# Lower halves of the k and v loads issued from GpSimd's queue instead of SyncE's

## Chip, cores and metric

The kernel runs on one core of a Trainium2 chip. The metric is the device time of one launch in microseconds (us); lower is better. A core has TensorE (PE in the profile), VectorE (DVE), ScalarE (ACT), GpSimd (POOL) and SyncE (SP). Each of the five has its own instruction queue, worked in order. A DMA is issued by an instruction in one of these queues; the transfer itself is done by the core's 16 DMA engines.

## The reference, cut to what matters

All inputs are bf16. There are 2048 tokens of D = 640 channels; x is `A_q`.

```python
# branch A: a long convolution over the tokens
k_shift = sum(k_pad[:, t:t+S, :] * shift_k[:, 3 - t] for t in range(4))
kv = k_shift * v
y  = irfft(rfft(pad(kv)) * rfft(pad(ssm_k)))[:S] + kv * ssm_D
a  = q * y
# branch B: a mixer over four shifted column groups, then an MLP
h  = gelu(layernorm(x) @ w1)          # 640 -> 640
x1 = x + shifted(h) @ w2
b  = x1 + gelu(layernorm(x1) @ w3) @ w4   # 640 -> 1536 -> 640
# the gate
g   = sigmoid((x * gate_w).sum(-1, keepdims=True))
out = g * a + (1 - g) * b
```

## The kernel before

**Work and tiling.** The 2048 tokens are cut into 16 slices s = 0 to 15 of 128 partitions. A partition of the lower half (0 to 63) and one of the upper half (64 to 127) hold different token ranges, so that a load of token rows is written as two DMAs of 64 partitions each. The helper `halves` (line 378) does this: it makes one task that issues the upper half (g = 1) and then the lower half (g = 0), both from SP (line 382). The loads of x (`ldx`), k (`ldk`), v (`ldv`), q (`ldq`) and most stores go through it.

**Branch A.** The shifted k times v is worked out on DVE in four groups of four slices, kv3, kv2, kv1, kv0 in this order (lines 870 to 894). A group has four taps (a product of a window of K with a row of shift_k, line 878), three sums (line 882) and the product with v (line 886, called kv3.v to kv0.v here), all on 128 x 2560 elements in bf16. K is one buffer of 19 slices that holds all of k: its pieces are loaded by `ldk15`, `ldk11`, `ldk7`, `ldk3` (lines 554 to 556; the number is the first of four slices) and two smaller loads. A group takes its windows from its own piece and the one ahead of it: kv3 from K15 and K11, kv2 from K11 and K7, kv1 from K7 and K3. The product with v is written back into K. v has one buffer for all four groups (slot 0 of VC, line 871), so that the load of V2 can only start when kv3.v has read V3, and so on: `ldv3` waits for nothing on DVE, `ldv2` waits for kv3.v, `ldv1` for kv2.v, `ldv0` for kv1.v. The long convolution is a two-step Fourier transform by matmuls: step 1 for the filter (h, line 911) and for kv (x, line 913), evictions of PSUM into FS (lines 387 and 389), stores to DRAM scratch (line 943), loads back (FX, line 957), step 2 (line 965), products (line 980), the way back (lines 993, 1005, 1019, 1031). Step 1 of kv for slices 0 to 3 is the last of its kind and needs kv0.v.

**Branch B.** Layernorm statistics of x (`st1`, DVE or ACT) and their last part on POOL (`rs1`, lines 594 to 597: a power of -0.5 among others), normalization (`nm1`, lines 601 and 631), transposes, w1 (lines 689, 693), gelu (706), w2 (715), x1 (722), then the second layernorm: sums of squares on ACT (`sq`, line 727), `ve2` (lines 775 to 777 on POOL, or 779 and 780 on DVE) and `st2` (lines 785 to 787, always POOL) per pair of slices, `nm2` (lines 601 and 603) per slice, a transposing DMA (`dt2`, line 808), w3 (817), gelu (824), w4 (833, 842), and the sum with the residual (850). The name st2.2 means st2 of the pair of slices 2 and 3; nm2.2 is the normalization of slice 2, and it needs st2.2.

**What sets the order.** Every piece of work is a task with the engine that it runs on, the buffers that it reads and writes, and what it takes from small pools. A string (`ORDER`, line 37) lists all task numbers by hand in the order in which they are emitted; an engine's queue holds its instructions in this order. Semaphore waits are put in from what each instruction reads and writes. DMAs issued from SP take eight completion semaphores in turn, so that an SP issue also waits until the one eight before it on SP has landed.

On POOL the order before is: constants, `rs1` for slices 5, 4, 1, 0, 14, 3, 2, 15, `cjp` (the copy at line 389 that brings shift_k into rows), `rs1` for 9, 7, 6, 8, `dfold` (line 865), `rs1` for 11, 12, 13, 10, then ve2.0, st2.0, ve2.2, st2.2, ve2.4, st2.4, ve2.6, st2.6, st2.10, st2.8, st2.14, ve2.12, st2.12. On DVE, nm2.2 stands directly behind kv3.v and ahead of the first tap of kv2; nm2.4 and nm2.7 stand behind kv0.v.

Of the kernel before, what the change touches and what calls it, by code (L numbers as in the profile page):

```python
# [83 lines left out]
class Plan:  # L84
# [13 lines left out]
    def add(self, name, eng, dur, fn, r=(), w=(), use=(), acq=(), rel=(), roles=(), after=(), mode=None, nbytes=0):  # L98
        eng = dict(eng) if isinstance(eng, dict) else {eng: dur}
        t = Task(len(self.tasks), name, eng, fn)  # L100
        t.mode, t.bytes, t.roles, t.after = mode, nbytes, roles, after
        t.kept = None
        t.acq = [(a, 1, a == "U") if isinstance(a, str) else a for a in acq]
        t.rel = [(x[0], x[1], x[2] if len(x) > 2 else None) for x in rel]
        for k in r:
            if k in self.writer:
                t.deps |= self.writer[k]
            self.readers.setdefault(k, set()).add(t.idx)
        for k in w:
            t.deps |= self.writer.get(k, set()) | self.readers.pop(k, set())  # L110
            self.writer[k] = {t.idx}
        for o in use:
            t.deps.add(o.idx)
        t.deps.discard(t.idx)
        self.tasks.append(t)
        return t
# [238 lines left out]
def build(env, nc, io):  # L355
# [22 lines left out]
    def halves(name, nbytes, out, in_, **kw):  # L378

        def fn(t):  # L380
            for g in (1, 0):
                nc.sync.dma_start(out=out(t, g), in_=in_(t, g))  # L382
        return add(name, "SP", 1.08, fn, nbytes=nbytes, **kw)

    def copy(t, out, in_):
# [115 lines left out]
    def c_bm(t):  # L501
        for g in range(2):
# [8 lines left out]
                                                  in_=io["sk"].rearrange("d j -> (d j)").unsqueeze(0)), w=["CJR"], roles=("VC",))  # L511
# [6 lines left out]
                                                           in_=env.CD[:].broadcast_to([P, 4 * D])), r=["CD"], w=["CJP"] + [("CJ", j) for j in range(4)], roles=("VC",))  # L518
# [20 lines left out]
    for s0, n in ((2, 2), (4, 2), (6, 4), (0, 2), (14, 2), (10, 4)):  # L539
        halves(f"ldx{s0}", P * n * D * BF * (HALF if n < 4 else 1.05), lambda t, g, s0=s0, n=n: env["x"][64 * g:64 * g + 64, s0:s0 + n, :],  # L540
               lambda t, g, s0=s0, n=n: qv[g, :, s0:s0 + n, :], w=[("x", s, g) for s in range(s0, s0 + n) for g in range(2)])
# [3 lines left out]
                                                     in_=io["w2"].rearrange("(q r) n -> r q n", q=4)[0:128]),  # L545
        w=["W2a"], roles=("W12",))
    for q in range(4):
        dma(f"ldw2b{q}", 40960, lambda t, q=q: nc.sync.dma_start(out=env["W12"][32 * q:32 * q + 32, 1, 4, :],
                                                                 in_=io["w2"][160 * q + 128:160 * q + 160, :]),
# [4 lines left out]
    for i0 in (15, 11, 7, 3):  # L554
        halves(f"ldk{i0}", P * 4 * D * BF * 1.05, lambda t, g, i0=i0: env["K"][64 * g:64 * g + 64, i0:i0 + 4, :],
               lambda t, g, i0=i0: kv_[g, :, i0 - 3:i0 + 1, :], w=[("K", i, g) for i in range(i0, i0 + 4) for g in range(2)], roles=("K",))
# [62 lines left out]
    for s0 in pairs:  # L619
# [16 lines left out]
        if s0 in DMA1:  # L636
            for s, n in zip((s0, s0 + 1), nm):
                dma(f"dt1.{s}", P * D * BF * 1.8, lambda t, s=s, n=n: nc.sync.dma_start_transpose(
                    out=env["xnT"][:, s + 2, :, :], in_=env["xn"][:, n.buf["xn"][0], :]), issue=1.25, use=[n], rel=[(n, "xn")],
# [29 lines left out]
    for G in (1, 0, 2, 3):  # L669
        a = 4 * G  # L670
        owner = None
        for part in (3, 1, 0, 2, 4) if G == 0 else (2, 0, 1, 3, 4):
# [6 lines left out]
            def w1(t, a=a, fbs=fbs):  # L679
# [6 lines left out]
                for b, fb in enumerate(fbs):  # L686
# [9 lines left out]
            t = add(f"w1.{G}.{part}", "PE", 1.1, w1, r=["W1"] + [("xnT", s) for s in sorted(need)] +  # L696
                    [("xnTz", z) for z in (-2, 16) if z in need or z + 1 in need], use=[owner] if owner else [], acq=[ONE] if owner else [ONE, "hs"],
                    mode="f" if part < 4 else "c32", roles=("xnT", "W12"))
# [11 lines left out]
        for s in range(a, a + 4):  # L710
            def w2(t, s=s, o=owner):
                m = env.Uf(t.buf["U"][0])
                for (c0, c1) in ((0, 512), (512, 640)):
# [3 lines left out]
            t = add(f"w2.{s}", "PE", 1.38, w2, r=["W2a"] + [("W2b", q) for q in range(4)] + [("hs", G, p) for p in range(5)],  # L717
                    rel=[(owner, "hs")], acq=("U",), mode="f", roles=("W12", "hsT"))
# [75 lines left out]
    for c in range(4):  # L794
# [18 lines left out]
        for fb in range(12):  # L813
            def w3(t, fb=fb, nP=nP):
                for kb in range(5):
# [3 lines left out]
            t = add(f"w3.{c}.{fb}", "PE", 1.09, w3, r=["W3"] + [("x1nT", 4 * c + i) for i in range(4)], rel=[(nT, nP)],  # L819
                    use=[h2] if h2 else [], acq=[ONE] if h2 else [ONE, "h2"], after=("xnT",), mode="c64" if c == 3 else "f")  # L820
# [5 lines left out]
        for s in range(4 * c, 4 * c + 4):  # L826
# [19 lines left out]
            t = add(f"w4.{s}", "PE", 3.28, w4, acq=("U",), **kw)  # L846
# [7 lines left out]
    for cb in range(5):  # L854
# [5 lines left out]
        t = add(f"trh.{cb}", "PE", 1.0, trh, r=["ID", ("SK", cb)], use=[fill], acq=("U",), mode="f", roles=("SK",))  # L860
# [9 lines left out]
    for gi in (3, 2, 1, 0):  # L870
        halves(f"ldv{gi}", P * 4 * D * BF * 1.05, lambda t, g: env["VC"][64 * g:64 * g + 64, 0, :, :],
               lambda t, g, gi=gi: vv[g, :, 4 * gi:4 * gi + 4, :], w=["V"], roles=("VC",))
# [79 lines left out]
    for m in range(10):  # L952
        own, e2 = {}, {}
        for which in "hx":
# [5 lines left out]
            for pc in range(2):  # L960
                def mm(t, ld=ld, pc=pc):
                    X = env["FX"][:, ld.buf["FX"][0], :]
                    for j in range(4):
# [5 lines left out]
                t = add(f"s2{which}.{m}.{pc}", "PE", 0.22, mm, use=[ld] + ([o] if o else []), r=["TRIG"], rel=[(ld, "FX")],  # L969
                        acq=("U",) if o else ("U", pool), mode="q32", after=("VC",), roles=("FX",))  # L970
# [24 lines left out]
        t = add(f"s3.{m}", "PE", 0.88, back, use=[pa, pb], rel=[(pa, "PP")], acq=[("U", 1, True), ("U", 1, True)], mode="s32", roles=("PP",))  # L995
# [19 lines left out]
        out=env["BT"][:], in_=env.BP.rearrange("p s t -> p (s t)")), issue=1.25, r=["BP"], w=["BT"])  # L1015
    for s0 in range(0, 16, 2):
        def rg(t, s0=s0):
# [4 lines left out]
                      lambda t, g, s0=s0: qv[g, :, s0:s0 + 2, :], acq=("Q",), w=[("q", s0)], after=("W12",))  # L1022
        oown = None
        for i in range(2):
# [8 lines left out]
            t = add(f"s4.{s}", "PE", 0.29, mm, use=[ld], r=["BT"], rel=[(ld, "GX")], acq=("U",), mode="c64")  # L1033
# [36 lines left out]
        if s0 in LATE:  # L1070
            continue
        halves(f"st.{s0}", P * 2 * D * BF * 1.3, lambda t, g, s0=s0: ov[g, :, s0:s0 + 2, :],
               lambda t, g, o=oown: env["QO"][64 * g:64 * g + 64, 4 + 2 * o.buf["O"][0]:6 + 2 * o.buf["O"][0], :],
# [33 lines left out]
```

## Time and profile before

| | us |
|---|---|
| median of 3 plain runs | 225.13 (224.52 to 225.18) |
| the profiled execution | 227.05 |
| its span, first to last instruction | 225.3 |
| ACT busy | 154.4 |
| POOL busy | 45.8 |
| idle ahead of DVE's first tap | 2.06 |

The profiled execution is one run, some 2 us longer than the median; the span leaves out what lies ahead of the first instruction and behind the last. TensorE's granted clock was 1.000 on this core. Over the whole span 57.94 MB are moved at a mean of 257 GB/s; SP's queue carries 57.27 MB of it in 39158 packets, 89.9% of the time of 16 DMA engines. POOL issues no DMA. In a row of a timeline the columns are the start, the time of the row (both in us), the engine, the line, the operation with what it writes and reads, the count, and in brackets the idle time ahead of it with what ended it. "SPq" is SP's queue, whose instructions are DMA issues; "us to landing" is the time from issue to landing. In the rows of stages, the columns behind an engine's busy time in brackets are instruction counts; the last three are TensorE's granted clock, the share of the 16 DMA engines' time, and GB/s.

### The profile page before, as it was taken

To read this page: it belongs to the slowest core of one execution; us is meant where nothing else is said; L and a number is where in the kernel's file an instruction comes from. 1 tells how busy PE (TensorE), PEld (TensorE's weight loads), DVE (VectorE), ACT (ScalarE), POOL (GpSimd) and SP (SyncE) were. 2 spreads that over 40 slices of the span, in tenths; PEclk is the share of its full clock that TensorE was granted. 3 is DMA by queue.
4 is the path that set the end of the run, shared out by engine and by line. 5 is a ranking of instruction groups with operands and counts; after the bars stand their busy time and mean duration, and the time that the engine had idled before them with its cause. 6 is when DMAs were issued, how large, how long until landed. Compare 5 with 4: busy or idle time off the path is not lost.

```text
span 225.3 us, 5381 instructions
## 1 busy us (share of the span) xinstructions
PE 212.7 (94%) x2161; PEld 106.4 (47%) x2178; DVE 189.3 (84%) x281; ACT 154.4 (69%) x225; POOL 45.8 (20%) x86
## 2 busy tenths in 40 slices
PE   3999889899999999999999999999999999999992
PEld 1576454466444444345543433334444555555561
DVE  7998896999999999997469989899857426989984
ACT  6998969799988999889658988888675002225000
POOL 7481532436200009930710000000000000000000
PEclk9999999999999999999999999999999999999999
DMA  6999999999999998979899989999992596988624
GB/s 193 281 308 232 220 237 238 327 233 327 349 240 287 241 272 252 379 270 270 193 367 311 373 154 285 316 304 309 247 255 88 185 374 209 281 250 249 203 64 116
DMA packets 39503, 57.94 MB, mean 257 GB/s; under 512 B 15027, under 2 KB 30645, under 8 KB 39478
## 3 DMA queue, kind: packets, MB, share of 16 engines
q1 hardware_dynamic: 39158, 57.27, 89.9%
q10 hardware_dynamic: 320, 0.33, 0.5%
q8 instruction: 17, 0.28, 0.5%
q14 instruction: 8, 0.07, 0.1%
HBM read 35.56 MB, written 18.36 MB: 239 GB/s over the span
## 4 chain that ended last, share of the span: by engine, by line
PE 63%; DMA 17%; DVE 12%; SPq 3%; issue 2%; ACT 1%; DVEq 0%
PE PS L817 18%; PE PS L833 17%; PE PS L715 9%; DMA x<-in_A_q_dram 7%; PE PS L965 5%; DMA W<-in_B_w_dram 4%; PE PS L689 4%; PE PS L993 4%; DMA SK<-in_A_ssm_k_dram 3%; DVE VC L878 3%; DVE VC L882 3%; DMA QO<-in_A_q_dram 2%; SPq L382 2%; PE PS L911 2%; PE PS L1031 1%
## 5 line engine op out<-in xcount | busy, mean ns | idle before, releaser
L824 ACT ACTIVATE h2T<-PS 128x512 bf16<-128x512 f32 x48 | 27.9, 605 | 27.3 <-PE PS L817 26.9
L833 PE MATMUL PS<-W,h2T 128*128 128x512 bf16 (+3 forms) x306 | 39.8, 298 | 0.3
L387 ACT CAST FS<-PS 128x1024 bf16<-128x1024 f32 x37 | 36.0, 1021 | 5.4 <-PE PS L913 3.5
L817 PEld LDWEIGHTS <-W 128*128 128x128 bf16 (+1 forms) x300 | 22.1, 103 | 29.4 <-issue 8.4
L833 PEld LDWEIGHTS <-h2T 128*128 128x128 bf16 (+1 forms) x312 | 22.4, 100 | 18.5 <-issue 1.6
L387 ACT CAST XH<-PS 128x1024 bf16<-128x1024 f32 x26 | 25.5, 1020 | 7.5 <-PE PS L965 7.4
L817 PE MATMUL PS<-x1nT,W 128*128 128x512 bf16 x120 | 28.5, 380 | 0.0
L817 PE MATMUL PS<-XB,W 128*64 128x512 bf16 (+1 forms) x180 | 28.5, 380 | 0.0
L980 DVE TENSOR_TENSOR PP<-XH 128x2048 bf16<-128x2048 bf16 x20 | 23.6, 1219 | 3.1 <-ACT XH L387 2.8
L878 DVE TENSOR_TENSOR VC<-K,VC 128x2560 bf16<-128x2560 bf16 x16 | 23.7, 1490 | 2.3 <-DMA W<-in_B_w_dram 2.1
L715 PE MATMUL PS<-W,hsT 128*128 128x128 bf16 (+1 forms) x155 | 23.5, 297 | 0.9 <-DMA W<-in_B_w_dram 0.6
L850 DVE TENSOR_TENSOR x<-PS,x 128x640 bf16<-128x640 f32 x12 | 9.8, 823 | 13.4 <-PE PS L833 13.2
L689 PE MATMUL PS<-xnT,W 128*128 128x512 bf16 x80 | 19.2, 379 | 0.1
L715 PEld LDWEIGHTS <-hsT 128*128 128x128 bf16 x160 | 12.8, 98 | 13.0 <-issue 1.1
L882 DVE TENSOR_TENSOR VC<-VC 128x2560 bf16<-128x2560 bf16 x12 | 17.9, 1489 | 0.3
L389 DVE CAST XH<-PS 128x1024 bf16<-128x1024 f32 x14 | 16.9, 1220 | 1.2 <-PE PS L965 1.1
L1037 DVE SCALAR_TENSOR_TENSOR W<-PS,GG,QO 128x640 bf16<-128x640 f32 x16 | 13.6, 877 | 2.4 <-PE PS L1031 1.9
L387 ACT CAST GS<-PS 128x1024 bf16<-128x1024 f32 x12 | 12.0, 1016 | 3.9 <-PE PS L993 3.9
L255 PE MATMUL PS<-C 128*128 128x512 bf16 x34 | 9.9, 434 | 3.8 <-DVE C L506 3.7
L842 PE MATMUL PS<-W,h2T 128*64 128x512 bf16 (+1 forms) x192 | 13.4, 299 | 0.0
L722 DVE SCALAR_TENSOR_TENSOR x<-PS,x 128x640 bf16<-128x640 f32 x16 | 12.8, 815 | 0.1
L965 PE MATMUL PS<-FX,TRIG 64*32 64x512 bf16 x320 | 12.4, 381 | 0.3 <-ACT GS L387 0.3
(115 smaller groups left out, 294.0 us busy)
## 6 DMA issues: line engine op xcount, KB each, us to landing
FH<-FS SPq DMA_DIRECT2D x8, 640.0 KB, 6.3
FXD<-FS SPq DMA_DIRECT2D x8, 640.0 KB, 5.0
FX<-FH SPq DMA_DIRECT2D x10, 512.0 KB, 6.0
FX<-FXD SPq DMA_DIRECT2D x10, 512.0 KB, 5.3
GX<-GD SPq DMA_DIRECT2D x8, 640.0 KB, 5.9
W<-in_B_w_dram SPq DMA_DIRECT2D x2, 1920.0 KB, 11.9
GD<-GS SPq DMA_DIRECT2D x8, 480.0 KB, 4.0
SK<-in_A_ssm_k_dram SPq DMA_DIRECT2D x5, 512.0 KB, 6.5
```

The source lines that it names most:

```text
L387: nc.scalar.copy(out=out, in_=in_)
L389: (nc.vector if t.on == "DVE" else nc.gpsimd).tensor_copy(out=out, in_=in_)
L689: nc.tensor.matmul(m[:, b, :], lhsT=W[:, 0, kb, 160 * fb:160 * fb + 128], rhs=rhs(kb, shifts[fb]), start=(kb == 0), stop=(kb == 4))
L715: nc.tensor.matmul(m[:, c0:c1], lhsT=env["hsT"][:, o.buf["hs"][0], fb, 128 * (s % 4):128 * (s % 4) + 128], rhs=env["W12"][:, 1, fb, c0:c1] ...
L817: nc.tensor.matmul(env.PS[q:q + w, t.buf["U"][0], :], lhsT=env["W3"][:, kb, 128 * fb + q:128 * fb + q + w], rhs=env.nT(int(nP[-1]))[:, :, ...
L824: nc.scalar.activation(out=env["h2T"][:, o.buf["h2"][0], fb, :], in_=env.PS[:, t.buf["U"][0], :], func=ACT.Gelu_apprx_tanh)
L833: nc.tensor.matmul(m[q:q + w, c0:c1], lhsT=env["h2T"][:, o.buf["h2"][0], fb, a:a + w], rhs=env["W4"][:, fb, c0:c1], start=(fb == 0), stop= ...
L878: nc.vector.tensor_tensor(out=VC[:, o], in0=env["K"][:, a + 3 - j:a + 7 - j, :], in1=w, op=ALU.mult)
L882: nc.vector.tensor_tensor(out=VC[:, 1], in0=VC[:, 1], in1=VC[:, 2], op=ALU.add)
L965: nc.tensor.matmul(env.U(t.buf["U"][0])[32 * j:32 * j + 32, gp, :], lhsT=CRI()[64 * gp:64 * gp + 64, 32 * pc:32 * pc + 32], rhs=X[64 * gp: ...
L980: nc.vector.tensor_tensor(out=env["PP"][:, o.buf["PP"][0], a, :].rearrange("p (b c) -> p b c", b=2), in0=X.unsqueeze(1).broadcast_to([P, 2 ...
L1037: nc.vector.scalar_tensor_tensor(out=u, in0=env.Uf(t.buf["U"][0])[:, 0:D], scalar=SS("GG")[:, s:s + 1], in1=env["QO"][:, 2 * q.buf["Q"][0] ...
```

## The change

The helper picks the queue by half and by the task's name: the lower half of a task whose name begins with `ldk` or `ldv` is issued from GpSimd's queue. The upper halves, and all other tasks of the helper, stay on SP.

```diff
         def fn(t):
             for g in (1, 0):
-                nc.sync.dma_start(out=out(t, g), in_=in_(t, g))
+                q = nc.gpsimd if g == 0 and name.startswith(("ldk", "ldv")) else nc.sync
+                q.dma_start(out=out(t, g), in_=in_(t, g))
         return add(name, "SP", 1.08, fn, nbytes=nbytes, **kw)
```

Eight DMAs move: the lower halves of K15, K11, K7, K3, V3, V2, V1 and V0, 320 KB each. The loads `ldkh0` and `ldkh1` (lines 557 to 563) don't go through the helper and stay. In `ORDER` nothing changes. On POOL the new issues come to stand so: K15 behind `cjp`, K11 between `rs1` of 7 and of 6, K7, V3 and K3 (in this order) between `rs1` of 10 and ve2.0, V2 between ve2.2 and st2.2, and V1 and V0 between st2.2 and ve2.4. V2, V1 and V0 wait for the same product on DVE as before. The numbers of lines behind 382 are one higher in the changed kernel.

## Prediction, on record before the change was run

> **What bounds the kernel now.** I read the page's busy shares first, then the busy time by stage, then the chain of work that ended last, then each engine's timeline where the moved issues stand.
>
> ```profile
> PE 212.7 (94%) x2161; PEld 106.4 (47%) x2178; DVE 189.3 (84%) x281; ACT 154.4 (69%) x225; POOL 45.8 (20%) x86
> ```
>
> ```profile
> core 0: us, PE busy (x) PEld busy (x) DVE busy (x) ACT busy (x) POOL busy (x), PEclk, DMA share, GB/s
> ...
> 20.00:40.60 20.60, 17.88 (x148) 8.87 (x147) 16.50 (x40) 17.40 (x29) 6.13 (x11) 1.00 1.00 240
> 40.60:57.60 17.00, 16.82 (x127) 9.77 (x130) 16.60 (x24) 14.65 (x24) 9.10 (x16) 1.00 1.03 294
> 57.60:98.10 40.50, 40.34 (x285) 17.81 (x287) 39.77 (x40) 36.37 (x55) 12.92 (x13) 1.00 1.00 280
> 98.10:114.40 16.30, 16.02 (x121) 8.82 (x122) 10.26 (x24) 11.74 (x23) 5.01 (x15) 1.00 0.97 267
> 114.40:207.00 92.60, 91.91 (x1147) 42.34 (x1152) 74.12 (x77) 56.47 (x74) 0.00 (x0) 1.00 0.91 266
> ```
>
> From 57.6 to 98.1 us two engines are full at once: PE works 40.34 of 40.50 us, DVE 39.77. After 98.1 PE has 0.28 + 0.69 us left idle until 207. So nothing there can take up a delay of PE; and up to 98.1 a delay of DVE stays on DVE. The chain says where the two meet.
>
> ```profile
> 30.95 9.63 DMA W<-in_B_w_dram
> ...
> 83.43 1.50 DVE K L886
> ...
> 94.77 1.50 DVE VC L882
> 96.30 1.49 DVE K L886
> ```
>
> The end hangs on W2's landing at 40.58, then on PE and DVE, with DVE's last two kv products (kv1.v and kv0.v, L886) on it. PE's transform of the first four slices (L913) needs that product:
>
> ```profile
> 98.09 0.83 PE L913 MATMUL PS<-K,TRIG 64*128 64x512 bf16 x12
> ```
>
> kv0.v ends at 96.30 + 1.49 = 97.79, L913 starts at 98.09. A DVE instruction is seen by another engine 0.04 us later (DVE ends 57.23 and SP issues 57.27, rows below), so PE's slack against kv0.v is 98.09 - 97.83 = 0.26 us. The profiled run took 227.05 us, its span 225.3; the median of the plain runs is 225.13. I work out a difference from the profiled execution and add it to 225.13.
>
> **The change, part by part.** Eight issues (the halves for partitions 0 to 63 of K15, K11, K7, K3 and V3, V2, V1, V0) go from SP to POOL, at the same places of the order. Bytes and landing places stay. A POOL issue with an unmet wait holds everything behind it on POOL, as a wait does now: the 26.60 us that L777 waits for ACT hold L785 behind it.
>
> *Price of one issue on POOL.* No POOL issue stands in this trace. Nearest rows, SP's issues of the same transfers:
>
> ```profile
> L382 SPq DMA_DIRECT2D K<-in_A_k_dram x8: 465/530/1393, 20.8 to 44.1; - x8
> ...
> L382 SPq DMA_DIRECT2D VC<-in_A_v_dram x8: 519/604/929, 42.1 to 85.6; - x8
> ```
>
> POOL's own instructions bound it: 0.20 (L786 below) to 2.54, the longest one.
>
> ```profile
> 15.38 2.54 POOL L389 COPY VC<-VC 1x2560 bf16<-1x2560 bf16 x1
> ```
>
> I take 0.93, the longest issue of a v half on SP; 0.20 and 2.54 are kept for the range.
>
> *The v half for group 2 is the step that costs.* It waits for kv3.v on DVE, since it overwrites what kv3.v reads. On POOL the three instructions of st2.2 (L785 to L787) come right behind it, and on DVE the normalization nm2.2 (L603), directly after kv3.v, needs their result. So kv3.v, then the issue, then st2.2, then nm2.2 become a line in which DVE stands still. Before, st2.2 ran beneath kv3.v:
>
> ```profile
> 53.72 1.95 POOL L785 TENSOR_TENSOR r<-v,MH 128x2 f32<-128x2 f32 x1 [0.17 <-POOL v L777]
> 55.75 1.55 POOL L786 TENSOR_TENSOR SB<-r,S 128x2 f32<-128x2 f32 x1
> 57.38 0.22 POOL L787 TENSOR_SCALAR SB<-SB 128x2 f32<-128x2 f32 x1
> ...
> 107.49 0.71 POOL L785 TENSOR_TENSOR r<-v,MH 128x2 f32<-128x2 f32 x1 [9.62 <-DVE v L779]
> 108.28 0.20 POOL L786 TENSOR_TENSOR SB<-r,S 128x2 f32<-128x2 f32 x1
> 108.56 0.22 POOL L787 TENSOR_SCALAR SB<-SB 128x2 f32<-128x2 f32 x1
> ```
>
> ```profile
> 53.61 1.48 DVE L878 TENSOR_TENSOR VC<-K,VC 128x2560 bf16<-128x2560 bf16 x1
> ...
> 55.75 1.48 DVE L886 TENSOR_TENSOR K<-VC 128x2560 bf16<-128x2560 bf16 x1
> 57.64 0.45 DVE L603 TENSOR_SCALAR xn<-x,r,SB 128x640 bf16<-128x640 bf16 x1 [0.40 <-POOL SB L787]
> 58.00 1.49 DVE L878 TENSOR_TENSOR VC<-K,VC 128x2560 bf16<-128x2560 bf16 x1
> ```
>
> ```profile
> 57.27 1.16 SPq L382 DMA_DIRECT2D VC<-in_A_v_dram x2
> ```
>
> Even before, DVE waited 0.40 here for POOL. With DVE idle, st2.2 takes 108.56 + 0.22 - 107.49 = 1.29 (beside kv3.v it took 3.88). New start of L603: 57.27 + 0.93 + 0.08 + 1.29 + 0.04 = 59.61 instead of 57.64: **+1.97** on DVE. Behind it stand all the taps of groups 2, 1 and 0, in the stage where DVE has hardly an idle moment. At L913 PE's slack takes 0.26: 1.97 - 0.26 = **+1.71**, for good. With 0.20 for the issue it is +0.98, with 2.54 it is +3.32. V2 itself lands by 57.27 + 0.93 + 9.0 = 67.2 (9.0 is the longest landing of a v half, row below) and is wanted after six more taps and sums of 1.5 from 58.00 + 1.97: 69.0.
>
> *K15 and K11, lower halves.* They leave at about 17.9 and 25.8 instead of between 20.8 and 27.5. The DMA share from 20 to 40.6 is 1.00: the same bytes stand ahead of W2, so its landing moves little. At most, PE wins the wait ahead of w2, and DVE the one ahead of its first tap; both rows say what was waited for.
>
> ```profile
> 40.63 2.89 PE L715 MATMUL PS<-W,hsT 128*128 128x512 bf16 x19 [0.59 <-DMA W<-in_B_w_dram]
> ...
> 38.45 2.89 DVE L878 TENSOR_TENSOR VC<-K,VC 128x2560 bf16<-128x2560 bf16 x2 [2.06 <-DMA W<-in_B_w_dram]
> ```
>
> Three instructions after that tap DVE needs w2's first output, so DVE's gain ends where PE's does: 0.59. In the other direction, one half (320 KB) passing x and SK at 240 GB/s costs 1.3 us. I take 0, with -0.59 and +1.3 as the ends. Behind K11 stand rs1.6 and rs1.8:
>
> ```profile
> 25.46 0.30 POOL L597 TENSOR_SCALAR NB<-SA,RS 128x1 f32<-128x1 f32 x1
> 26.10 0.57 POOL L595 TENSOR_TENSOR RS<-VE,MH 128x1 f32<-128x1 f32 x1 [0.34 <-DVE SA L581]
> ```
>
> ```profile
> 26.73 1.22 DVE L389 COPY HT<-PS 128x2048 bf16<-128x2048 bf16 x1 [0.65 <-PE PS L859]
> ```
>
> The issue ends at 25.76 + 0.93 = 26.7, so rs1.6 ends 0.6 later, at 27.3; DVE is in its copy until 27.95 and normalizes after it. That copy is the cover; without it, 0.6.
>
> *K7, V3, K3, lower halves.* On POOL they stand behind the last rs1, and ahead of ve2.0:
>
> ```profile
> 43.66 1.53 POOL L597 TENSOR_SCALAR NB<-SA,RS 128x1 f32<-128x1 f32 x1
> 47.99 0.20 POOL L775 TENSOR_TENSOR v<-S 128x2 f32<-128x2 f32 x1 [2.80 <-DVE x L722]
> ```
>
> 45.19 + 3 x 0.93 = 47.98: ve2.0 is not held. POOL next waits for kv3.v at 57.27 and had done ve2.2 at 53.56, so 3.7 us cover more. K7 is wanted by the tap at 53.61, V3 by kv3.v at 55.75. Landing of these pieces before (K7, V3, K3 in three windows):
>
> ```profile
> K<-in_A_k_dram SPq DMA_DIRECT2D x2, 320.0 KB, 6.9
> ...
> VC<-in_A_v_dram SPq DMA_DIRECT2D x2, 320.0 KB, 7.6
> ...
> K<-in_A_k_dram SPq DMA_DIRECT2D x2, 320.0 KB, 9.2
> ```
>
> K7 done at 45.19 + 0.93 + 6.9 = 53.0, V3 at 46.12 + 0.93 + 7.6 = 54.7: both in time, K7 by 0.6 only. I take 0; with 9.2 for K7 it is 55.3 and DVE loses 1.7, which adds to the above.
>
> *V1 and V0, lower halves.* V1 goes when kv2.v ends and is wanted seven taps and sums later, 10.4 us against 0.93 + 9.0. V0 goes when kv1.v ends, 84.93 + 1.97 = 86.90, and lands by 96.8 at the latest, wanted at 96.30 + 1.97 = 98.27. Both are in time. But ve2.4, st2.4, ve2.6 and st2.6 now stand behind V0:
>
> ```profile
> DMA to landing us min/median/max: 5.4/6.6/9.0
> ```
>
> ```profile
> 84.74 0.24 POOL L777 TENSOR_TENSOR v<-v,S 128x2 f32<-128x2 f32 x1 [26.60 <-ACT JK L727]
> ...
> 96.41 1.46 POOL L787 TENSOR_SCALAR SB<-SB 128x2 f32<-128x2 f32 x1
> ...
> 100.80 0.43 DVE L603 TENSOR_SCALAR xn<-x,r,SB 128x640 bf16<-128x640 bf16 x1
> ```
>
> The ten instructions took 84.74 to 97.87, most of them stretched to about 1.5 beside the taps. Two more come (L775, L776, which ran early before). From 87.83, seven at 1.5 reach 98.3, one ends with the taps at 97.79 + 1.97 = 99.8, the other four take 1.6 (0.28 and, by the rows of st2 above, 1.29): 101.4. DVE's use (nm2.7) is at 100.80 + 1.97 = 102.8. Hidden by 1.4 us; with 2.54 for the issue, 1.0 of that cover is left, and whatever goes beyond it is lost on DVE.
>
> *SP* saves eight issues of some 0.57 us and their places in its rotation, but its stores wait for ACT and DVE, so this is worth nothing.
>
> **Sum**: +1.71, so 225.13 + 1.7 = **226.8 us**.
>
> **The rivals.**
> (1) *Not slower.* If the v half's wait doesn't stop POOL, st2.2 runs beneath kv3.v as before, the 1.97 is gone, and the head's 0.59 is left: 224.5. It would need POOL to pass a waiting issue; the 26.60 us row speaks against it. It decides at nm2.2: it would start within some 0.4 us of kv3.v's end. For more than -0.59 the head would have to fill more of the 2.72 us that PE idles from 20 to 40.6; only a part of that waits for loads. I give 0.13 to no change (within 0.3%, about what can be told from no change here) and 0.12 to faster.
> (2) *K7 is late.* It decides from a landing over 53.61 - 46.12 = 7.5 us: with 9.2 it gives 225.13 + 1.7 + 1.7 = 228.5. For: 6.9, 7.6 and 9.2 straddle it. Against: SP's queue holds three halves fewer ahead of it.
> (3) *POOL's issue is held by DVE.* POOL's small instructions go from 0.20 to 1.5 beside taps. If an issue can't proceed beside taps at all, V0 goes only when kv0's last sum ends, at 96.27 + 1.97 = 98.24, lands 0.93 + 5.4 (the shortest landing) later at 104.6, and kv0.v slips by 6.3: 225.13 + 1.7 + 6.3 = 233.1. Held for one tap only (1.49), K7 lands at 53.0 + 1.5 = 54.5 and DVE loses 0.9: 227.7. For: the stretched rows. Against: those instructions read SBUF, and an issue has no tensor to read.
>
> The Trainium skill bears on (3) (SBUF — State Buffer, "A bandwidth-pool intuition that's wrong" and the box before it): descriptors of a GpSimd DMA can't be written while DVE holds the shared ports, 620 ns becoming 3100. Its "Who interferes with whom" says that a tensor_tensor keeps GpSimd from reading only, not from writing, which would spare these issues. No run here shows which holds; by the first, the time would be rival (3)'s.
>
> **How the numbers follow.** Forecast 0.56 (+0.4 to +3.3), K7 late or held for one tap 0.14, held long 0.05, no change 0.13, faster 0.12. The range leaves out most of faster and of held long: 225.0 to 229.7, the upper end being the sum with 2.54 for the issue plus the head's +1.3. Faster 0.12, same 0.13, slower 0.75.
>
> **What would show it.** Right: DVE idle of some 2 us ahead of L603 after kv3.v, put down to POOL; st2.2's three instructions short; PE idle of about 1.5 us ahead of L913 near 98. K7 late: idle ahead of the tap at 53.6, put down to a DMA. Held: POOL's issues of 1.5 us and more, kv0.v waiting for its v. Wrong: no idle at L603, or a POOL issue so dear (over 2.5 us) that st2.6 comes too late for DVE at 102.8.

## The result, and the profile after

The changed kernel took **227.59 us** in the median of 8 runs (226.20 to 231.37), the kernel before 225.16 in 8 runs beside it. The ratio is **1.0085, with a 95% interval of 1.0055 to 1.0114**: some 1.9 us slower, against a forecast of +1.7 us (226.8). Every ratio here leaves out disturbed runs, such as the one of 231.37, while the medians hold all runs, and so lie 2.4 us apart here. The profiled run of the changed kernel took 228.07 us, its span is 226.3 us, and the mean granted clock 0.998.

The busy shares of the changed kernel's page hardly move; POOL has eight instructions more, the issues:

```profile
PE 212.5 (94%) x2161; PEld 106.4 (47%) x2178; DVE 189.7 (84%) x281; ACT 154.7 (68%) x225; POOL 47.0 (21%) x94
```

The table of stages says where the time went: from 57.6 to 98.1 us PE works 38.69 us where it worked 40.34, with the granted clock still at 1.00.

```profile
57.60:98.10 40.50, 38.69 (x276) 17.23 (x278) 38.45 (x38) 34.92 (x52) 12.66 (x16) 1.00 0.98 274
```

The place is found on three timelines, POOL's, DVE's and PE's (start, time, engine, line, operation; in brackets the idle time ahead and what ended it; line numbers are one higher than before). POOL:

```profile
52.76 0.20 POOL L778 TENSOR_TENSOR v<-v,S 128x2 f32<-128x2 f32 x1 [1.83 <-ACT JK L728]
57.00 0.62 POOL L383 DMA_DIRECT2D VC<-in_A_v_dram  x1 [4.05 <-DVE K L887]
57.64 0.75 POOL L786 TENSOR_TENSOR r<-v,MH 128x2 f32<-128x2 f32 x1
58.47 0.20 POOL L787 TENSOR_TENSOR SB<-r,S 128x2 f32<-128x2 f32 x1
58.76 0.23 POOL L788 TENSOR_SCALAR SB<-SB 128x2 f32<-128x2 f32 x1
```

DVE:

```profile
55.22 1.49 DVE L887 TENSOR_TENSOR K<-VC 128x2560 bf16<-128x2560 bf16 x1
59.02 0.45 DVE L604 TENSOR_SCALAR xn<-x,r,SB 128x640 bf16<-128x640 bf16 x1 [2.32 <-POOL SB L788]
```

PE:

```profile
73.75 1.52 PE L716 MATMUL PS<-W,hsT 128*128 128x512 bf16 x9 [1.66 <-DVE x L723]
...
99.42 0.83 PE L914 MATMUL PS<-K,TRIG 64*128 64x512 bf16 x12
```

POOL has what st2.2 needs at 52.96 and stands still for 4.05 us on V2's issue, because that issue waits for kv3.v. kv3.v ends at 55.22 + 1.49 = 56.71; then come the issue (57.00 to 57.62), st2.2 (57.64 to 58.99) and nm2.2 (59.02). DVE's wait at nm2.2 is 2.32 us where it was 0.40: +1.92. Some 13 us later PE stands still for 1.66 us: the row names DVE's x1 (L723) as what w2 waited for, and x1 is what reads w2's output out of PSUM, so w2 waited for a place there. In the kernel before, the same matmuls followed without a gap (PE's timeline):

```profile
71.88 0.61 PE L913 MATMUL PS<-K,TRIG 64*128 64x512 bf16 x4
72.41 1.53 PE L715 MATMUL PS<-W,hsT 128*128 128x512 bf16 x9
```

Up to there PE was 0.39 us ahead of before (71.49 against 71.88 at the L914 matmuls ahead of it). From there on it is about 1.3 us later (73.75 against 72.41; 99.42 against 98.09), and nothing up to 207 us takes that back. In these two profiles a part is taken back at the end: DVE's timeline of before has two waits there for DMAs, of 0.26 and 0.48 us, and after the change DVE comes late enough to have neither.

```profile
212.39 1.68 DVE L1064 SCALAR_TENSOR_TENSOR QO<-x,OG,W 128x640 bf16<-128x640 bf16 x2 [0.26 <-DMA out_dram<-QO]
214.55 0.88 DVE L1037 SCALAR_TENSOR_TENSOR W<-PS,GG,QO 128x640 bf16<-128x640 f32 x1 [0.48 <-DMA QO<-in_A_q_dram]
```

The two profiled spans differ by 1.0 us only (226.3 against 225.3). The profiled run of before was one of its longer ones: 25 other runs of it, taken later, have a median span of 223.4 us. Single profiles are therefore read for mechanisms here, and times come from the repeated runs.

### The profile page after: what moved, and what is told of

It reads as the page before. It is cut to its first block, busy times and chain, and to the rows that moved or that the text cites. A ratio compares the mean times of both kernels' runs of the same rounds, so it can differ in the third digit from the quotient of the medians.

```text
span 226.3 us, 5385 instructions
## 1 busy us (share of the span) xinstructions
PE 212.5 (94%) x2161; PEld 106.4 (47%) x2178; DVE 189.7 (84%) x281; ACT 154.7 (68%) x225; POOL 47.0 (21%) x94
## 4 chain that ended last, share of the span: by engine, by line
PE 46%; DVE 21%; DMA 18%; issue 5%; SPq 5%; ACT 3%; POOL 1%; DVEq 0%
PE PS L818 16%; PE PS L834 12%; DMA W<-in_B_w_dram 8%; DVE VC L879 6%; DVE VC L883 6%; PE PS L843 5%; DMA CD<-VC 5%; DVE x L723 4%; DMA FX<-FXD 4%; PE PS L994 4%; PE PS L966 4%; DVE K L887 3%; PE PS L716 2%; SPq L383 2%; PE PS L1032 2%
## 5 line engine op out<-in xcount | busy, mean ns | idle before, releaser
L723 DVE SCALAR_TENSOR_TENSOR x<-PS,x 128x640 bf16<-128x640 f32 x16 | 12.9, 820 | 1.0 <-PE PS L716 0.7
```

The lines of the kernel that those rows point to most:

```text
L723: nc.vector.scalar_tensor_tensor(out=x, in0=env.Uf(t.buf["U"][0])[:, 0:D], scalar=1.0, in1=x, op0=ALU.mult, op1=ALU.add, accum_out=SS("S1" ...
```

## The experiments

Two explanations stood against each other. **Hold**: V2's issue alone does it, because it waits on POOL ahead of st2.2. **Queue**: two DMA queues side by side cost time in themselves, through the order in which pieces land or POOL's late start. The diffs are cut to the lines that differ from the changed kernel; the line that issues stays as it is there. Each ratio is taken to runs of the kernel before on the same chip. Three chips were used, on which its medians were 225.16, 225.40 and 225.91 us.

### V2 alone, all but V2, V2 behind st2.2

```diff
-q = nc.gpsimd if g == 0 and name.startswith(("ldk", "ldv")) else nc.sync
+q = nc.gpsimd if g == 0 and name == "ldv2" else nc.sync
```

> Only the lower half of V2 goes from GpSimd's queue, the other seven stay on SP. Theory (the hold at nm2.2 is the loss, the rest of the change a small gain ahead of it): DVE idles 2.3 us ahead of nm2.2 as after the change, PE loses 1.3 to 1.9 in the middle, and without the 0.5 us that the first pieces won the time is before + 1.5 to 2.1 us, 226.7 to 227.3. Rival (eight loads on a second queue cost time as such, by sharing the DMA engines): one load in eight, so before + 0.3 or less, 225.5 at most.

```diff
+q = nc.gpsimd if g == 0 and name.startswith(("ldk", "ldv")) and name != "ldv2" else nc.sync
```

> Seven lower halves on GpSimd's queue, V2's on SP. Theory: st2.2 runs beneath kv3.v again, DVE idles 0.4 us or less ahead of nm2.2, the head's gain of 0.5 us is left: 224.3 to 225.2, not slower than before. Rival (second queue costs as such): 7/8 of the loss stays, 226.5 to 227.

```diff
+if q is nc.gpsimd and name == "ldv2":
+    env.held = lambda t=t, g=g: nc.gpsimd.dma_start(out=out(t, g), in_=in_(t, g))
+    continue
...
 # at the end of st2
+if s0 == 2:
+    env.held()
```

> All eight lower halves on GpSimd's queue, but V2's is issued behind st2.2 instead of ahead of it: same loads, same queue, same number of issues, only the place of one. Theory: as with V2 on SP, 224.3 to 225.2, DVE idle of 0.4 us or less ahead of nm2.2. Rival (second queue): as after the change, 226.5 to 227.5.

Measured: V2 alone 229.96 us, ratio 1.0203 [1.0160, 1.0246]; all but V2 226.15, ratio 1.0031 [0.9997, 1.0065]; V2 behind st2.2 226.53, ratio 1.0068 [1.0038, 1.0098]. Both kernels without the hold missed their expectation, which was not slower than before. But DVE's wait at nm2.2 is back at 0.40 us in both, and PE has no stop near 73 us. DVE's timeline, with all but V2 on POOL:

```profile
55.59 0.45 DVE L604 TENSOR_SCALAR xn<-x,r,SB 128x640 bf16<-128x640 bf16 x1 [0.40 <-POOL SB L788]
```

and with V2 behind st2.2:

```profile
56.40 0.45 DVE L607 TENSOR_SCALAR xn<-x,r,SB 128x640 bf16<-128x640 bf16 x1 [0.40 <-POOL SB L791]
```

So the wait is the hold's work. But by the medians the time of before isn't reached again without it, and V2 alone is *slower* than all eight. The latter needs a reason of its own. POOL, DVE and PE of the kernel with V2 alone:

```profile
51.17 0.20 POOL L778 TENSOR_TENSOR v<-v,S 128x2 f32<-128x2 f32 x1 [1.84 <-ACT JK L728]
56.75 0.77 POOL L383 DMA_DIRECT2D VC<-in_A_v_dram  x1 [5.38 <-issue]
```

```profile
53.63 1.49 DVE L887 TENSOR_TENSOR K<-VC 128x2560 bf16<-128x2560 bf16 x1
58.92 0.45 DVE L604 TENSOR_SCALAR xn<-x,r,SB 128x640 bf16<-128x640 bf16 x1 [3.80 <-POOL SB L788]
```

```profile
73.65 1.87 PE L716 MATMUL PS<-W,hsT 128*128 128x512 bf16 x10 [3.14 <-DVE x L723]
```

kv3.v ends at 55.12, but POOL's issue starts at 56.75, 1.63 us later; among the eight it starts 0.29 us later. PE's idle time grows to 3.14 us, and behind it the granted clock falls to half (table of stages, columns PE, PEld, DVE, ACT, POOL, granted clock, DMA share, GB/s):

```profile
73.00:74.00 1.00, 0.35 (x2) 0.19 (x2) 1.00 (x3) 0.00 (x0) 0.00 (x0) 1.00 1.22 325
74.00:75.00 1.00, 1.00 (x8) 0.51 (x6) 1.00 (x3) 0.00 (x0) 0.00 (x0) 0.83 1.14 246
75.00:76.00 1.00, 1.00 (x8) 0.37 (x6) 1.00 (x2) 0.00 (x0) 0.00 (x0) 0.50 0.81 172
76.00:77.00 1.00, 1.00 (x5) 0.41 (x4) 1.00 (x3) 0.90 (x1) 0.00 (x0) 0.50 1.31 138
77.00:78.00 1.00, 1.00 (x4) 0.29 (x2) 0.90 (x1) 0.84 (x3) 0.00 (x0) 0.50 0.91 192
78.00:79.00 1.00, 1.00 (x16) 0.55 (x14) 0.36 (x1) 0.04 (x1) 0.00 (x0) 0.96 0.00 0
```

The missing clock adds up to 0.17 + 3 x 0.50 + 0.04 = 1.71 us of PE time. The fall isn't sure to come: of the six runs of this kernel, two had a mean clock of 0.999 and took 228.01 and 228.31 us, one had 0.993 (this profile, 229.31), and three had 0.985 and took 230.61 to 231.33. Two new theories follow: the first DMA that POOL issues in a launch starts late when it comes behind a wait, and a PE idle time of some 3 us costs clock on top.

### K15 and K11 apart from the other six

```diff
+q = nc.gpsimd if g == 0 and name in ("ldk15", "ldk11") else nc.sync
```

> Only the lower halves of K15 and K11 on GpSimd's queue. Theory (these two let SP send W2 and the taps' coefficients sooner): the head's gain of 0.4 to 0.6 us alone, kv3's first tap starts 1 to 2 us sooner, w2 some 0.4 us sooner: 224.5 to 224.9. Rival (the head's gain is scatter of one run, or comes from K7, V3, K3): 225.1 to 225.3 and w2 at 40.6 as before.

Six others, K15 and K11 on SP:

```diff
+q = nc.gpsimd if g == 0 and name in ("ldk7", "ldk3", "ldv3", "ldv2", "ldv1", "ldv0") else nc.sync
```

> Six lower halves on GpSimd's queue, all but K15 and K11, V2's still ahead of st2.2. Theory (two costs: the hold at nm2.2, about 1.9 us, and up to 0.7 us more in the head from K15 and K11 jumping ahead of x and SK): the hold alone, DVE idle of 2.2 to 2.4 us ahead of nm2.2, before + 1.3 to 1.9: 226.5 to 227.1. Rival (loads on a second queue cost in proportion to their number): 3/4 of the change's 1.9, 226.6, and no difference to the kernel with V2 behind st2.2.

The same six, with V2's issue behind st2.2 as above:

> The same six on GpSimd's queue, V2's behind st2.2. Theory: neither of the two costs is left: 225.0 to 225.6, DVE idle 0.4 us ahead of nm2.2, no PE idle near 73. Rival (second queue as such): 226.3 to 226.9, as with V2 ahead of st2.2.

K15 and K11 alone, K15's issue held back to the place of K11's:

```diff
+q = nc.gpsimd if g == 0 and name in ("ldk15", "ldk11") else nc.sync
+if q is nc.gpsimd and name == "ldk15":
+    env.held = lambda t=t, g=g: nc.gpsimd.dma_start(out=out(t, g), in_=in_(t, g))
+    continue
+if q is nc.gpsimd and name == "ldk11":
+    env.held()
```

> Lower halves of K15 and K11 on GpSimd's queue, K15's held back to K11's place, some 7 us later than in the kernel with these two (225.7, before + 0.3%). Theory (K15 issued at 18 us gets between the x, SK and B-matrix loads that PE and ACT wait for): its loss goes, 225.0 to 225.4. Rival (the loss is that of a second queue's traffic, wherever it falls): 225.6 to 225.9.

Measured: K15 and K11 alone 225.73 us, ratio 1.0030 [1.0006, 1.0054]; the six 226.74, ratio 1.0062 [1.0033, 1.0090]; the six with V2 behind st2.2 **225.43, ratio 1.0000 [0.9970, 1.0029]**; K15 held back 226.21, ratio 1.0032 [0.9995, 1.0070].

The pair of the six settles the hold: one issue moved behind three small instructions takes 226.74 - 225.43 = 1.3 us away, and with it the whole loss. A second queue for the six costs nothing by itself that the interval of 0.3% would show. DVE and PE of the six:

```profile
58.11 0.45 DVE L604 TENSOR_SCALAR xn<-x,r,SB 128x640 bf16<-128x640 bf16 x1 [2.31 <-POOL SB L788]
```

```profile
72.84 1.52 PE L716 MATMUL PS<-W,hsT 128*128 128x512 bf16 x9 [1.64 <-DVE x L723]
```

With V2 behind st2.2, POOL's timeline shows st2.2 (L789 to L791 there) done at 55.04, before kv3.v even starts (55.34), and the issue behind both:

```profile
53.14 0.72 POOL L789 TENSOR_TENSOR r<-v,MH 128x2 f32<-128x2 f32 x1
53.94 0.79 POOL L790 TENSOR_TENSOR SB<-r,S 128x2 f32<-128x2 f32 x1
54.82 0.22 POOL L791 TENSOR_SCALAR SB<-SB 128x2 f32<-128x2 f32 x1
57.12 0.62 POOL L384 DMA_DIRECT2D VC<-in_A_v_dram  x1 [2.08 <-DVE K L892]
```

Among the eight, by the ratios, the same move takes only 1.0085 - 1.0068 = 0.0017 away, with intervals of 0.003 on both. What each part costs behind kv3.v can be read from the profiles: take kv3.v's end from the span. That leaves 167.6 to 168.1 us in all six profiles without the hold (before, all but V2, V2 behind st2.2 with eight and with six, K15 and K11 alone in both forms), and 169.4 to 169.6 us in the four with a wait of 2.31 to 2.35 us at nm2.2. So the hold costs 1.4 to 2.0 us there, with eight loads on POOL (169.6 against 168.0) as with six, and whatever K15 and K11 cost lies ahead of kv3.v's end. There single profiles scatter too much to show it: kv3.v ends between 55.1 and 57.9 us.

K15 and K11 are the rest. Alone they cost about 0.3% (0.7 us); all eight are 1.0085 - 1.0062 = 0.0023 above the six, and with V2 behind st2.2 the eight are 1.0068 - 1.0000 = 0.0068 (1.5 us) above the six. The differences are of the size of the intervals, but every pair leans the same way. That K15's early place is the cause, as expected, isn't borne out: held back by 7 us, the pair had nearly the same ratio (1.0032), though its interval takes in 1.0000 too.

One lead is in SP's timelines. SP stores the taps' coefficients to DRAM (CD<-VC), must wait until they have landed, reads them back for all partitions (VC<-CD), and only then issues w2's loads. K15 and K11 alone:

```profile
19.16 0.26 SPq L516 DMA_DIRECT2D CD<-VC  x1
...
29.68 0.34 SPq L518 DMA_DIRECT2D VC<-CD  x1
```

before:

```profile
19.39 0.26 SPq L515 DMA_DIRECT2D CD<-VC  x1
...
27.94 0.34 SPq L517 DMA_DIRECT2D VC<-CD  x1
```

Rid of two issues, SP gets to the read-back sooner, but then stands there for the store: 5.6 to 7.9 us in the five profiles with both on POOL, 3.6 us at most in the seven with both on SP. It sent the first of w2's loads at 27.5 to 30.1 us in the five, at 26.8 to 29.6 in the seven: not sooner, as the expectation for the two had supposed. Whether this delay is the 0.3%, no run shows; the cause stays open.

### The first DMA on POOL, and more issues in the hold

K15 and V2 alone (K15 as POOL's first DMA):

```diff
+q = nc.gpsimd if g == 0 and name in ("ldk15", "ldv2") else nc.sync
```

> Lower halves of K15 and V2 on GpSimd's queue: V2's alone gave before + 4.6 us, and its issue came 1.63 us after kv3.v where it comes 0.3 us after it in the changed kernel. Theory (the first DMA that GpSimd issues in a launch costs some 1.3 us more; V2's was the first there): with K15 ahead the issue comes 0.3 us after kv3.v, DVE idles 2.2 to 2.4 us instead of 3.8, PE's idle near 73 is 1.5 to 2.0 instead of 3.1, the clock stays at 1.00 there, and the time is 226.7 to 227.5. Rival (the 1.63 us comes from the wait on V3's landing on SP's semaphore): 229.5 to 230.5 as with V2 alone.

V2 alone, with a row of 1.3 KB as POOL's first DMA:

```diff
+q = nc.gpsimd if g == 0 and name == "ldv2" else nc.sync
...
-dma("ldD", 2048, lambda t: nc.sync.dma_start(
+dma("ldD", 2048, lambda t: nc.gpsimd.dma_start(
```

> V2's lower half alone on POOL, as in the kernel that took 229.96 us, and the row of ssm_D (1.3 KB, early in the kernel) issued from POOL too, so that V2's isn't POOL's first DMA. Theory: the first DMA that POOL issues in a launch starts some 1.3 us later than the ones behind it when it has had to wait; then V2's issue starts 0.3 us behind kv3.v's end instead of 1.63, DVE's wait ahead of nm2.2 is 2.3 instead of 3.80, the granted clock stays at 1.00 near 74 us, and the time is 227.0 to 227.5. Rival: the delay belongs to the first large transfer (K15 took it away in the run with K15 and V2) or to the place; then the wait stays at 3.8 and the time near 230.

The six, V2's lower half in four issues:

```diff
+if name == "ldv2" and g == 0:
+    for j in range(4):
+        q.dma_start(out=out(t, g)[:, j:j + 1, :], in_=in_(t, g)[:, j:j + 1, :])
+    continue
```

> The six lower halves on POOL as in the kernel that took 226.74 us, with V2's lower half cut into four issues of one slice each, one behind the other on POOL. Theory (the hold): every issue between kv3.v and st2.2 adds its own time to DVE's wait ahead of nm2.2. With 0.52 for each further issue (V3's and K3's in that kernel) the wait goes from 2.31 to 3.8 us, PE's idle time ahead of w2 near 73 us from 1.64 to 3.1, and the time by 1.3 to about 228.0. If it was PE's idle time of 3.14 us that pulled the granted clock down in the run with V2 alone, the clock falls here too, in the 4 us behind the idle time, and the time is nearer 229. Rival A: the fall there came of the late first DMA and not of the idle time; then the clock stays at 1.00 and the time at 228.0. Rival B: POOL's issues overlap with the instructions behind them, so that the wait stays near 2.3 and the time at 226.7.

The six, with both halves of V2 on POOL:

```diff
+q = nc.gpsimd if name == "ldv2" or g == 0 and name in ("ldk7", "ldk3", "ldv3", "ldv1", "ldv0") else nc.sync
```

> As the six lower halves on POOL, with V2's upper half on POOL as well, ahead of its lower half. Theory (the hold): one more issue of 0.52 to 0.62 us between kv3.v and st2.2: DVE's wait ahead of nm2.2 goes from 2.31 to 2.85, PE's idle time near 73 us from 1.64 to 2.2, the time from 226.74 to about 227.2. The clock stays at 1.00 if the fall needs more than that, and shows a fall if it begins at 2 us. Rival: the wait is a fixed price of POOL's waking and not of the issue's length; then it stays at 2.3 and the time at 226.7.

With the small first DMA, V2's issue starts 0.31 us behind kv3.v (54.37 + 1.49 = 55.86), and DVE's wait is 2.35. POOL and DVE of that kernel:

```profile
12.26 0.75 POOL L521 DMA_DIRECT2D C<-in_A_ssm_D_dram  x1
...
56.17 0.64 POOL L383 DMA_DIRECT2D VC<-in_A_v_dram  x1 [2.40 <-DVE K L887]
```

```profile
54.37 1.49 DVE L887 TENSOR_TENSOR K<-VC 128x2560 bf16<-128x2560 bf16 x1
58.20 0.45 DVE L604 TENSOR_SCALAR xn<-x,r,SB 128x640 bf16<-128x640 bf16 x1 [2.35 <-POOL SB L788]
```

It took 227.42 us, ratio 1.0072 [1.0036, 1.0108], against 1.0203 without the small one; K15 as the first gave 227.89, ratio 1.0120 [1.0079, 1.0162]. In both, V2 still follows V3's landing on SP's queue, so that rival for the 1.63 us falls. So the late start belongs to being the first, not to size or place.

The kernel with four issues has POOL at them for 2.18 us, and what hangs on them grows as expected:

```profile
55.97 2.18 POOL L385 DMA_DIRECT2D VC<-in_A_v_dram  x4 [2.39 <-DVE K L891]
```

```profile
59.54 0.45 DVE L608 TENSOR_SCALAR xn<-x,r,SB 128x640 bf16<-128x640 bf16 x1 [3.87 <-POOL SB L792]
```

```profile
74.27 0.58 PE L720 MATMUL PS<-W,hsT 128*128 128x512 bf16 x1 [3.20 <-DVE x L727]
```

```profile
74.00:78.00 4.00, 3.50 (x14) 1.48 (x15) 3.23 (x8) 0.34 (x1) 0.00 (x0) 0.57 0.97 213
```

Here V2's issue isn't POOL's first, the idle time is as long as with V2 alone, and the clock falls in the same way: the fall goes with the idle time. One of the six runs kept a mean clock of 0.999, two had 0.985. The time, 230.66 us, is above the 229 expected. Both halves of V2 on POOL gave the wait that was expected (2.82) but a longer PE idle time (2.43 for 2.2), and 228.85 us for 227.2:

```profile
60.68 0.45 DVE L604 TENSOR_SCALAR xn<-x,r,SB 128x640 bf16<-128x640 bf16 x1 [2.82 <-POOL SB L788]
```

```profile
75.41 1.52 PE L716 MATMUL PS<-W,hsT 128*128 128x512 bf16 x9 [2.43 <-DVE x L723]
```

The profiled run kept a clock of 1.00 behind that idle time. Of the other eleven runs, two had a mean clock of 1.000 and took 226.56 and 226.87 us; nine had 0.992 or 0.993 and took 228.68 us and more. A loss of 1.71 of some 225 us is 0.0076, so 0.992 fits one such fall; no profile shows it in this kernel.

| on POOL | DVE's wait at nm2.2, us | PE idle near 73 us, us | clock behind it | span less kv3.v's end, us | ratio |
|---|---|---|---|---|---|
| six, V2 behind st2.2 | none | none | 1.00 | 167.6 | 1.0000 [0.9970, 1.0029] |
| six | 2.31 | 1.64 | 1.00 | 169.6 | 1.0062 [1.0033, 1.0090] |
| all eight (the change) | 2.32 | 1.66 | 1.00 | 169.6 | 1.0085 [1.0055, 1.0114] |
| V2, small first DMA | 2.35 | 1.67 | 1.00 | 169.4 | 1.0072 [1.0036, 1.0108] |
| K15 and V2 | 2.33 | 1.66 | 1.00 | 169.4 | 1.0120 [1.0079, 1.0162] |
| six, both halves of V2 | 2.82 | 2.43 | 1.00 in the profile | 169.8 | 1.0111 [1.0071, 1.0152] |
| V2 alone | 3.80 | 3.14 | 0.58 | 172.4 | 1.0203 [1.0160, 1.0246] |
| six, V2 in four | 3.87 | 3.20 | 0.57 | 172.1 | 1.0202 [1.0150, 1.0255] |

In all rows with a wait but that of both halves, PE's idle time is the wait less 0.66 to 0.68: DVE may be that late, counted from no wait at all, before PE notices. No version beat the kernel before.

## Why the prediction held, point by point

- **The line kv3.v, issue, st2.2, nm2.2** came as forecast: 2.31 us from kv3.v's end to nm2.2's start, forecast 59.61 - 57.23 = 2.38; +1.92 on DVE, forecast +1.97. The pair of the six shows that it causes the loss of the six; in the change's 1.9 us the cost of K15 and K11 is added to it.
- **The price of an issue**, taken as 0.93, was a sum of two things: POOL starts the issue 0.29 us after kv3.v's end, and the issue takes 0.62. SP's upper half of the same task was issued 0.02 us after kv3.v's end in the same profile. The forecast put 0.04 for the start, as on SP, and was right only because it took the longest issue of SP.

```profile
56.73 0.52 SPq L383 DMA_DIRECT2D VC<-in_A_v_dram  x1
```

- **Where PE feels it** was wrong. The forecast had PE's slack at L913 near 98 us and an idle time of 1.5 us there. PE stopped at 73.75 at w2, through PSUM, and had no wait at L914: kv0.v ended at 97.59 + 1.49 = 99.08, L914 started at 99.42, as far apart as before (0.34 and 0.30). The size came out alike, since 1.92 - 1.66 = 0.26 was free at w2 too; that the two slacks agree is chance.

```profile
97.59 1.49 DVE L887 TENSOR_TENSOR K<-VC 128x2560 bf16<-128x2560 bf16 x1
```

- **That the loss is for good** is borne out: PE is still 1.6 us later at 207 us (L1032 at 207.88 against 206.30). The waits of before at the end, shown above, take some of it back in that pair of profiles only: the six have 1.7 us of such waits there, with V2 behind st2.2 they have 0.6.
- **K15 and K11** were the term that was mis-sized: taken at nothing within -0.59 to +1.3, they cost 0.5 to 1.5 us by the pairs above. The reason given, that the same bytes stand ahead of W2, left out SP's wait for the store of the coefficients; whether that is the cost stays open. The hold, forecast at +1.71, is +1.4 by the ratio of the six (0.0062 x 225.4) and 1.4 to 2.0 us by the profiles. That the sum came so near to the forecast is in part luck, since the hold alone had been given all of it.
- **K7, V3 and K3** landed in time: in the changed kernel DVE has no wait for them, so rival 2 falls. Three other kernels had a wait of 0.23 to 0.47 us for V2, at kv2.v.
- **V1 and V0** are hidden. V0's issue took 0.51 us beside a tap (DVE is in one from 86.29 to 87.78), and st2.6 ended at 100.23, ahead of nm2.7 at 102.09. POOL's timeline of the changed kernel:

```profile
86.55 0.51 POOL L383 DMA_DIRECT2D VC<-in_A_v_dram  x1 [15.61 <-DVE K L887]
...
88.47 2.04 POOL L786 TENSOR_TENSOR r<-v,MH 128x2 f32<-128x2 f32 x1
90.58 0.92 POOL L787 TENSOR_TENSOR SB<-r,S 128x2 f32<-128x2 f32 x1
91.59 1.46 POOL L788 TENSOR_SCALAR SB<-SB 128x2 f32<-128x2 f32 x1
...
100.01 0.22 POOL L788 TENSOR_SCALAR SB<-SB 128x2 f32<-128x2 f32 x1
```

- **Rival 3** falls by the same rows: beside the taps, POOL's instructions that read a tensor are stretched up to 2.04 us, the issue, at 0.51, isn't. The Trainium skill says this under "Who interferes with whom" (SBUF — State Buffer): a tensor_tensor with both inputs in SBUF keeps GpSimd from reading, not from writing. The trace agrees with its 0.51 us. The 3100 ns that the same page gives for a GpSimd DMA beside a tensor_copy on DVE is not seen in any run here: no single issue took over 0.78 us.
- **Rival 1** (POOL passes a waiting issue) falls with the 4.05 us in which POOL had st2.2's inputs and did nothing.

## What to carry to other kernels

Before an issue with a wait goes to a compute engine's queue, look at what stands behind it there, and who waits for that: the cost is set by that chain and not by the issue. Here one position, ahead of or behind three instructions of 1.3 us together, decided between +1.3 us and nothing for the six loads. When a stall is added up to the bound engine, search for the first place where it is met; buffers passed back through PSUM may meet it before the data do.

## What the runs showed of the hardware

- **Start of an issue that waits.** POOL starts a DMA issue 0.29 to 0.31 us after the DVE instruction that it waits for ends; SP does it within 0.02 to 0.04 us. It isn't only the news from DVE: with V2 behind st2.2 among the eight, kv3.v had ended 0.63 us before, and the issue still came 0.27 us behind POOL's own last instruction.
- **First DMA.** The first DMA that POOL issues in a launch takes 0.75 to 0.78 us, later ones 0.51 to 0.64; standing behind a wait, the first one started 1.63 us after its releaser instead of 0.3 (one profile). Where POOL had been busy right up to it (K7 in the kernel with the six), no such gap was seen. What is done in that time, no trace shows.
- **Clock.** PE idle for 1.64 to 1.67 us leaves the granted clock at 1.00; idle for 3.14 or 3.20 us is followed in the profiles by some 3.4 us at 0.50, which is 1.7 us of PE time on top of the idle time. By their mean clocks, three of the twelve runs of these two kernels had no such fall, while of 77 runs of the kernel before only two were under 0.995; what decides it, no trace shows. The Trainium skill (TensorE: Matmul & The Clock Gate, "HAM oscillation — how this bites in real kernels") warns of gaps over about 3.4 us; its half clock and its window of 3.4 us agree with these rows, but here gaps somewhat shorter were enough.
- **Scatter of the head.** In the 13 profiles of this case DVE's first tap started between 35.7 and 39.1 us; with K15 and K11 alone on POOL it was 38.38, with K15's issue held back 36.19, though the two kernels' ratios are 1.0030 and 1.0032. A gain or loss of a microsecond there can't be read from one profile.
